# Long convolution with a routed MLP: who applies the filter's decay, products of ones ahead of the first data, and a small first chunk

## The chip, the cores and the metric

One core of one Trainium2 chip runs the program. The metric is the device time of an execution in microseconds (us); less is better. The engines are TensorE (PE in the rows; PEld is its weight load), VectorE (DVE), ScalarE (ACT), GpSimd (POOL) and SyncE (SP), which issues the DMAs.

## What is computed

The reference has two parts. The change lies in the first lines of the first one: the implicit filter.

```python
def _attn_ref(x, v, pos_emb, w1, w2):
    B, S, D = x.shape                                   # 4, 12608, 128
    h_mlp = np.maximum(pos_emb @ w1, 0.0) @ w2          # 64 -> 64 -> 128
    window = np.exp(-0.01 * np.arange(S))[:, None]
    h_filt = h_mlp * window
    u = x * v
    Uf = np.fft.rfft(u, n=2 * S, axis=1)
    Hf = np.fft.rfft(h_filt, n=2 * S, axis=0)
    y = np.fft.irfft(Uf * Hf[None], n=2 * S, axis=1)[:, :S]
    return x * y
```

The second part scores every row of that result with a gate vector, takes the 128 best rows of each batch, sends them through a ReLU MLP (128 to 1024 to 128), scales by the sigmoid of the score and adds them back.

## The kernel before, in words

The positions are laid out on a grid of 111 x 115 (partition, column), so that the transforms become products with small tables of cosines and sines. All products are float32, each of which the trace shows as two MATMUL instructions. The program has four stages: the filter layers (`h_hid`), the filter's spectrum (`h_spec`, 32 groups of four channels, written to a DRAM scratch `hd`), the main loop over 4 x 32 groups with the inverse transform and the row scores, and the routed MLP that runs as background work and at the end.

The order of work is written by hand: each engine runs its instructions in the order in which the code issues them, and the framework adds semaphore waits where two engines touch the same buffer.

`h_hid` is what the change touches. `pos` holds the position embeddings of column j in partitions 0 to 63 and of column j + 58 in partitions 64 to 127, so one product with the block-diagonal table `bw` (L275) makes the hidden layer of both halves. The 58 column pairs are cut into chunks of `PC = 4`: 14 whole chunks and a last one of two. For each chunk:

- L275, PE: first layer, 128 x 444, into one of two PSUM banks (`ps1(k % 2)`, named `a` in the rows).
- L276, ACT: Relu from that bank into `hid`.
- L284, PE: second layer, one product per column and half (64 rows deep, 111 x 128), into a PSUM tile of two banks, `ps2(k % 2)`, named `c`: the first bank for the lower half, the second for the upper.
- L293 and L297, DVE: for the lower half, the product with the decay (plane e = 0 of `hb`) and with the decay and a sign (plane e = 1). `hb` lies in `big` as [111, 2, 128, 115]: column j of a channel is 115 floats from column j of the next.
- L293, DVE, and L295, POOL: for the upper half, DVE makes plane 0, and POOL makes plane 1 from plane 0 with the sign.

The loop issues the first layer and the Relu of chunk k ahead of the second layer and multiplies of chunk k - 1. The DMAs of all chunks are issued at the start on SP's queue (L253), with the tables between them. Ahead of `h_hid`, DVE clears the PSUM banks (L723).

The spectrum begins with `fwd(0)` (`s1`, L228 by way of `mm2`, L221 and L222): 16 products on plane 0 for the lower and upper half, then 16 on plane 1. They need the last chunk's multiplies, on plane 1 those of POOL.

Of the kernel before, what the change touches and what calls it, by code (L numbers as in the profile page):

```python
# [11 lines left out]
AF = mybir.ActivationFunctionType  # L12
ALU = mybir.AluOpType
# [4 lines left out]
B, S, D, FO = 4, 12608, 128, 64  # L18
NQ = 64
N1, N2, N3 = 111, 230, 115  # L20
# [20 lines left out]
PJ = (N3 + 1) // 2  # L41
NC = 2
NS, ND = 64, 4
NWARM = 12
CB = range(2, (NJ + 7) // 8)
PC = 4
# [86 lines left out]
def hyena_moe(ctx, tc, xg, x2, pos, bw, ww, wg, mw1, mw2, c1, gx, cf, ci, wm, tk, out):  # L133
    nc = tc.nc
# [9 lines left out]
    def view(t, off, shape):  # L144
        n = int(np.prod(shape[1:]))
        r = t[:shape[0], off:off + n]
        if len(shape) > 2:
            ax = "abcd"[:len(shape) - 1]
            r = r.rearrange(f"p ({' '.join(ax)}) -> p {' '.join(ax)}", **dict(zip(ax[1:], shape[2:])))
        return r  # L150
# [8 lines left out]
    bank1 = [pp.tile([128, 512], F32, tag=f"a{k}", name=f"a{k}") for k in range(4)]  # L159
    bank2 = [pp.tile([128, 1024], F32, tag=f"c{k}", name=f"c{k}") for k in range(2)]  # L160

    def ps1(k, shape, name):
        return view(bank1[k], 0, shape)

    def ps2(k, shape, name):
        return view(bank2[k], 0, shape)
# [9 lines left out]
    wm_sb = cp.tile([N1, 3, N3], F32, name="wm_sb")  # L176
# [11 lines left out]
    onesb = cp.tile([128, 128], BF16, name="onesb")  # L188
    nc.vector.memset(onesb, 1.0)
    ay = view(big, 0, [128, NG, 2 * NJ, 4])  # L190
    hb = view(big, 0, [N1, 2, D, N3])
# [9 lines left out]
    def load_u(t):  # L201
        b, g = divmod(t, NG)
        if b < B:
            nc.sync.dma_start(buf("u", t, [NP, 2 * XC]), xg[b, :, g])
# [39 lines left out]
    def h_hid():  # L244
        pt, hid = view(arena, POS0, [128, PJ, N1]), view(arena, HID0, [128, PJ, N1])
        wl = view(big, D * 2 * NJ - 256, [128, 2, 128])
        bwt, wwt = wl[:, 0], wl[:, 1]
        nc.sync.dma_start(bwt, bw)
        ch = [(a, min(a + PC, PJ)) for a in range(0, PJ, PC)]

        def load(k):
            a, z = ch[k]
            nc.sync.dma_start(pt[:, a:z], pos[:, a:z])  # L253

        load(0)
        load(1)
        nc.sync.dma_start(wwt, ww)
        nc.sync.dma_start(wm_sb, wm)
        for k in range(2, 5):
            load(k)  # L260
        nc.sync.dma_start(c1_sb, c1)
        nc.sync.dma_start(cf_sb, cf)
        for k in range(5, len(ch)):
            load(k)
        nc.sync.dma_start(ci_sb, ci)
        nc.sync.dma_start(gx_sb, gx)
        nc.sync.dma_start(wgb, wg.partition_broadcast(128))
        nc.sync.dma_start(tk_sb, tk)
        for k in range(NU - 1):
            load_u(k)  # L270
        for k in range(len(ch) + 1):
            if k < len(ch):
                a, z = ch[k]
                hp = ps1(k % 2, [128, PC * N1], f"hid_{k}")[:, :(z - a) * N1]
                nc.tensor.matmul(hp, lhsT=bwt, rhs=pt[:, a:z].rearrange("p j i -> p (j i)"), start=True, stop=True)  # L275
                nc.scalar.activation(out=hid[:, a:z].rearrange("p j i -> p (j i)"), in_=hp, func=AF.Relu)  # L276
            if not k:
                continue
            a, z = ch[k - 1]
            ps = ps2(k % 2, [N1, 2, PC, D], f"hm_{k}")  # L280
            for i in range(z - a):
                for h in range(2):
                    if h * PJ + a + i < N3:
                        nc.tensor.matmul(ps[:, h, i], lhsT=hid[h * FO:(h + 1) * FO, a + i],  # L284
                                         rhs=wwt[h * FO:(h + 1) * FO], start=True, stop=True)
            for h in range(2):
                j0 = h * PJ + a
                j1 = min(h * PJ + z, N3)
                w = j1 - j0
                o = hb[:, :, :, j0:j1]  # L290
                pv = ps[:, h, :w].rearrange("p j d -> p d j")
                wb = wm_sb[:, :, j0:j1].unsqueeze(2).to_broadcast([N1, 3, D, w])
                nc.vector.tensor_tensor(out=o[:, 0], in0=pv, in1=wb[:, 0], op=ALU.mult)  # L293
                if h:
                    nc.gpsimd.tensor_tensor(out=o[:, 1], in0=o[:, 0], in1=wb[:, 1], op=ALU.mult)  # L295
                else:
                    nc.vector.tensor_tensor(out=o[:, 1], in0=pv, in1=wb[:, 2], op=ALU.mult)  # L297

    def h_spec():
        te = {}  # L300
# [363 lines left out]
    def moe(b, ix, ws, mb, ks):  # L664
# [11 lines left out]
        if b + 1 == B:  # L676
            wp = ps1(1, [128, 128], "warm")
            for _ in range(NWARM):
                nc.tensor.matmul(wp, lhsT=ident, rhs=ident, start=True, stop=True)
# [39 lines left out]
        ix = yield from place(b, rk, oh, jio, NJ, 3, ws[:, :128])  # L719
        yield from moe(b, ix, ws, mb, (3, (3, 3, 1, 2)[b]))  # L720

    for t in bank1 + bank2:
        nc.vector.memset(t, 0.0)  # L723
    h_hid()
    o, n, w = OFF["xa"]
    nc.gpsimd.memset(view(arena, o, [128, n * w]), 0.0)
# [7 lines left out]
    for t in range(NT + LAG):  # L734
        g = t % NG
        i = t - LAG
        if 0 <= i:
            f_i(i, sd.pop(i))
        if t < NT:
            p = ps1(2, [128, 512], f"p_{t}")  # L740
# [71 lines left out]
def build(inputs):  # L812
    import concourse.bacc as _bacc
    nc = _bacc.Bacc("TRN2", target_bir_lowering=False, num_devices=1, dynamic_dma_scratch_size=8192)
    arrays, args = {}, []
    for name, a in _layout(inputs):
        arrays[f"in_{name}_dram"] = a
        args.append(nc.dram_tensor(f"in_{name}_dram", a.shape, mybir.dt.from_np(a.dtype), kind="ExternalInput").ap())
    args.append(nc.dram_tensor("out_0_dram", (B, 2 * PR, NJ, D), F32, kind="ExternalOutput").ap())
    with tile.TileContext(nc) as tc:  # L820
        hyena_moe(tc, *args)
    return nc, arrays
# [7 lines left out]
```

## Time and profile before

| | us |
|---|---|
| three runs, median (range) | 1029.34 (1027.65 to 1029.87) |
| the profiled execution | 1029.24 |
| its span, first to last instruction | 1027.3 |
| busy PE / DVE / ACT / POOL | 955.7 / 907.7 / 596.5 / 673.2 |
| mean granted TensorE clock | 0.977 of full |

The profile is of one execution, and the prediction's sums are made against that one. A row of the timeline gives start, duration, engine, line, operation, output and input with shapes, a count when equal instructions that follow each other are merged, and in brackets the idle time before it with what ended it. Starts of instructions on one engine can lie closer than their durations, because the next one begins while the last is still writing. Matmul ends are modelled.

### The profile page before, as it was taken

How to read it: one execution, taken by the hardware profiler on the slowest of the kernel's cores; microseconds unless marked ns; L12 is line 12 of the kernel's file. 1: busy time of each engine (PE TensorE's matmuls, PEld its weight loads, DVE VectorE, ACT ScalarE, POOL GpSimd, SP SyncE). 2: the span in 40 equal slices, each digit the busy share in tenths (PEclk: the TensorE clock that was granted, in tenths of full speed). 3: DMA queues.
4: the chain of work that ended last, by engine and by line, in shares of the span. 5: the costliest groups of instructions: out<-in, count | busy, mean ns of one | idle time of the engine just before them, and what ended most of it. 6: DMA issues, size and time to landing. Idle time of an engine off the chain costs nothing.

```text
span 1027.3 us, 38294 instructions
## 1 busy us (share of the span) xinstructions
PE 955.7 (93%) x15812; PEld 850.5 (83%) x15812; DVE 907.7 (88%) x1559; ACT 596.5 (58%) x1957; POOL 673.2 (66%) x644
## 2 busy tenths in 40 slices
PE   8999989999999999999999999999999999889914
PEld 4788879988888988888889988888899888779903
DVE  7687879999999899999998899999988999996984
ACT  2344435545546887854557878644578876435810
POOL 4800018889887568988975598889845988863500
PEclk9999999999999999999999999999999999999956
DMA  8043366566785866656868765568587655554820
GB/s 234 22 160 152 153 210 199 176 180 196 200 231 180 268 196 179 194 172 184 232 210 270 202 190 172 173 183 243 186 271 220 185 171 178 164 170 127 296 74 5
DMA packets 64785, 190.26 MB, mean 185 GB/s; under 512 B 8693, under 2 KB 15716, under 8 KB 64612
## 3 DMA queue, kind: packets, MB, share of 16 engines
q1 hardware_dynamic: 64356, 187.30, 59.4%
q8 instruction: 124, 2.03, 0.9%
q0 software_dynamic: 256, 0.52, 0.2%
q14 instruction: 49, 0.40, 0.1%
HBM read 146.37 MB, written 41.42 MB: 183 GB/s over the span
## 4 chain that ended last, share of the span: by engine, by line
DVE 47%; PE 39%; issue 6%; DMA 2%; ACT 1%; DVEq 1%; POOLq 0%; SPq 0%; ACTq 0%
PE a L238 10%; PE a L221 9%; DVE arena L348 8%; DVE c L349 8%; PE c L221 7%; DVE c L341 5%; DVE c L340 5%; DVE arena L351 4%; DVE arena L417 4%; PE a L409 4%; DVE arena L350 4%; DVE arena L420 4%; PE a L222 3%; PE c L222 3%; PE c L238 2%
## 5 line engine op out<-in xcount | busy, mean ns | idle before, releaser
L238 PE MATMUL a<-arena,cf_sb 128*64 128x222 f32 x2304 | 260.3, 355 | 15.2 <-DVE c L341 14.3
L357 POOL TENSOR_TENSOR arena<-arena 128x444 f32<-128x444 f32 x127 | 133.7, 1052 | 198.5 <-DVE arena L351 132.4
L230 ACT COPY arena<-a 128x444 f32<-128x444 f32 x288 | 152.2, 530 | 161.5 <-PE a L222 158.5
L221 PE MATMUL c<-ci_sb,arena 128*56 128x116 f32 x2048 | 224.8, 263 | 3.7 <-DVE arena L351 2.5
L222 PE MATMUL c<-ci_sb,arena 128*55 128x116 f32 x2048 | 224.8, 263 | 0.0
L221 PE MATMUL a<-c_sb,arena 111*58 111x111 f32 x2048 | 218.3, 260 | 0.0
L238 PEld LDWEIGHTS a<-arena,cf_sb 128*64 128x64 f32 x2304 | 154.0, 137 | 77.7 <-DVE c L341 46.1
L222 PE MATMUL a<-c_sb,arena 111*57 111x111 f32 x2048 | 218.2, 260 | 0.0
L221 PEld LDWEIGHTS c<-ci_sb,arena 128*56 128x56 f32 x2048 | 207.1, 130 | 4.0 <-issue 2.7
L221 PEld LDWEIGHTS a<-c_sb,arena 111*58 111x58 f32 x2048 | 200.5, 132 | 10.0
L222 PEld LDWEIGHTS c<-ci_sb,arena 128*55 128x55 f32 x2048 | 206.9, 129 | 0.4 <-issue 0.4
L222 PEld LDWEIGHTS a<-c_sb,arena 111*57 111x57 f32 x2048 | 200.4, 131 | 0.2
L409 PE MATMUL a<-big,gx_sb 128*64 128x128 f32 x2880 | 169.8, 273 | 4.5 <-DVE arena L417 3.0
L434 ACT ACTIVATE arena<-arena 128x128 f32<-128x128 f32 x464 | 137.8, 298 | 60.8 <-DVE arena L420 54.7
L409 PEld LDWEIGHTS a<-big,gx_sb 128*64 128x64 f32 x2880 | 159.3, 137 | 8.4 <-DVE arena L417 5.5
L367 ACT COPY big<-c 128x928 f32<-128x928 f32 x128 | 118.3, 924 | 75.1 <-PE c L222 75.1
L210 POOL TENSOR_TENSOR arena<-arena 111x460 f32<-111x460 f32 x128 | 151.4, 1183 | 0.6 <-DMA arena<-in_xg_dram 0.6
L211 POOL TENSOR_TENSOR arena<-arena,wm_sb 111x460 f32<-111x460 f32 x128 | 140.4, 1097 | 10.0
L348 DVE TENSOR_TENSOR arena<-c,arena 128x888 f32<-128x888 f32 x128 | 138.5, 1082 | 7.7 <-DMA arena<-hd 3.4
L349 DVE TENSOR_TENSOR c<-c,arena 128x888 f32<-128x888 f32 x128 | 138.3, 1080 | 0.0
L358 POOL TENSOR_TENSOR arena<-arena 128x444 f32<-128x444 f32 x127 | 135.1, 1064 | 0.0
L393 POOL TENSOR_TENSOR arena<-big 128x256 f32<-128x256 f32 x104 | 90.9, 897 | 65.7 <-PE a L404 64.2
(130 smaller groups left out, 1532.0 us busy)
## 6 DMA issues: line engine op xcount, KB each, us to landing
arena<-hd SPq DMA_DIRECT2D x128, 444.0 KB
arena<-in_xg_dram SPq DMA_DIRECT2D x128, 402.5 KB
arena<-in_x_dram SPq DMA_DIRECT2D x112, 224.0 KB
out_dram<-arena SPq DMA_DIRECT2D x112, 224.0 KB
hd<-arena SPq DMA_DIRECT2D x32, 444.0 KB
arena<-in_moe_w_dram SPq DMA_DIRECT2D x8, 512.0 KB
arena<-in_pos_dram SPq DMA_DIRECT2D x14, 222.0 KB
arena<-in_x_dram SPq DMA_DIRECT2D x8, 112.0 KB
```

What stands on the lines that cost most here:

```text
L210: nc.gpsimd.tensor_tensor(out=u[:, 0], in0=u[:, 0], in1=u[:, 1], op=ALU.mult)
L211: nc.gpsimd.tensor_tensor(out=u[:, 1].rearrange("p (s j) -> p s j", s=4), in0=u[:, 0].rearrange("p (s j) -> p s j", s=4), in1=sg, op=ALU.mult)
L221: nc.tensor.matmul(o[:h], lhsT=lhsT[:, :h], rhs=rhs, **kw)
L222: nc.tensor.matmul(o[NQ:NQ + m - h], lhsT=lhsT[:, h:], rhs=rhs, **kw)
L230: nc.scalar.copy(out=te[:, e], in_=tps[e])
L238: nc.tensor.matmul(pq[w][e * NQ:(e + 1) * NQ, c], lhsT=cf_sb[:, 2 * w + e], rhs=te[:, e, c], start=True, stop=True)
L348: nc.vector.tensor_tensor(out=mt, in0=uv, in1=ht[:, 0].unsqueeze(1).to_broadcast([128, 2, HC]), op=ALU.mult)
L349: nc.vector.tensor_tensor(out=uv, in0=uv, in1=ht[:, 1].unsqueeze(1).to_broadcast([128, 2, HC]), op=ALU.mult)
L357: eng.tensor_tensor(out=nat(sd[:, 0]), in0=nat(yz[:, 0]), in1=rev(yz[:, 1]), op=ALU.add)
L358: eng.tensor_tensor(out=nat(sd[:, 1]), in0=rev(yz[:, 0]), in1=nat(yz[:, 1]), op=ALU.subtract)
L409: nc.tensor.matmul(ps[t * NQ:(t + 1) * NQ, k], lhsT=gx_sb[:, o:o + NQ], rhs=ay[:, :, e * NJ + j], start=e == 0, stop=e == 1)
L434: nc.scalar.activation(out=wx[:, k], in_=wx[:, k], func=AF.Copy, accum_out=self.sc[:, ja + k:ja + k + 1])
```

## The change

The decay of the upper half moves from DVE to ACT. ACT's activation takes one scale per partition, so it handles one column at a time: four instructions per chunk (three in the last). The multiplies of the lower half stay on DVE, POOL still makes plane 1 of the upper half. Ahead of the first chunk PE runs `NWARM0 = 24` products of a bfloat16 tile of ones into bank 3. The chunks are cut so that the first has two columns and the last is whole. For the first chunk the second layer is issued ahead of the next first layer. The clearing of the PSUM banks begins with bank 3.

```diff
+NWARM0 = 24
-        ch = [(a, min(a + PC, PJ)) for a in range(0, PJ, PC)]
+        ch = [(max(a, 0), a + PC) for a in range(PJ % PC - PC, PJ, PC)]
...
-        for k in range(len(ch) + 1):
+        def first(k):
             if k < len(ch):
                 a, z = ch[k]
                 hp = ps1(k % 2, [128, PC * N1], f"hid_{k}")[:, :(z - a) * N1]
                 nc.tensor.matmul(hp, lhsT=bwt, rhs=pt[:, a:z].rearrange("p j i -> p (j i)"), start=True, stop=True)
                 nc.scalar.activation(out=hid[:, a:z].rearrange("p j i -> p (j i)"), in_=hp, func=AF.Relu)
-            if not k:
-                continue
-            a, z = ch[k - 1]
+
+        wp = ps1(3, [128, 128], "warm0")
+        for _ in range(NWARM0):
+            nc.tensor.matmul(wp, lhsT=onesb, rhs=onesb, start=True, stop=True)
+        first(0)
+        for k, (a, z) in enumerate(ch):
+            if k:
+                first(k + 1)
             ps = ps2(k % 2, [N1, 2, PC, D], f"hm_{k}")
...
-            for h in range(2):
-                j0 = h * PJ + a
-                j1 = min(h * PJ + z, N3)
-                w = j1 - j0
-                o = hb[:, :, :, j0:j1]
-                pv = ps[:, h, :w].rearrange("p j d -> p d j")
-                wb = wm_sb[:, :, j0:j1].unsqueeze(2).to_broadcast([N1, 3, D, w])
-                nc.vector.tensor_tensor(out=o[:, 0], in0=pv, in1=wb[:, 0], op=ALU.mult)
-                if h:
-                    nc.gpsimd.tensor_tensor(out=o[:, 1], in0=o[:, 0], in1=wb[:, 1], op=ALU.mult)
-                else:
-                    nc.vector.tensor_tensor(out=o[:, 1], in0=pv, in1=wb[:, 2], op=ALU.mult)
+            if not k:
+                first(1)
+            w = min(PJ + z, N3) - PJ - a
+            o = hb[:, :, :, a:z]
+            pv = ps[:, 0, :z - a].rearrange("p j d -> p d j")
+            wb = wm_sb[:, :, a:z].unsqueeze(2).to_broadcast([N1, 3, D, z - a])
+            for e in range(2):
+                nc.vector.tensor_tensor(out=o[:, e], in0=pv, in1=wb[:, 2 * e], op=ALU.mult)
+            o = hb[:, :, :, PJ + a:PJ + a + w]
+            for i in range(w):
+                nc.scalar.activation(out=o[:, 0, :, i], in_=ps[:, 1, i], func=AF.Copy,
+                                     scale=wm_sb[:, 0, PJ + a + i:PJ + a + i + 1])
+            wb = wm_sb[:, 1, PJ + a:PJ + a + w].unsqueeze(1).to_broadcast([N1, D, w])
+            nc.gpsimd.tensor_tensor(out=o[:, 1], in0=o[:, 0], in1=wb, op=ALU.mult)
...
-    for t in bank1 + bank2:
+    for t in bank1[3:] + bank1[:3] + bank2:
         nc.vector.memset(t, 0.0)
```

In the changed kernel the first layer is L276, the Relu L277, the products of ones L281, the second layer L290, DVE's multiplies L299, ACT's scaling L302 and POOL's product L305.

How the order changes on ACT, from its first Relu on, with the semaphores that each instruction waits for (`PE_49`, `DVE_49`, `Activation_49` are raised by that engine, `DMAHW...` by a DMA; `a0`, `a1` are the banks of the first layer, `c0`, `c1` the tiles of the second). Before:

```order
L187 ACTIVATE gp_90<-one_88 128x1 [waits DVE_49]
L276 ACTIVATE arena_68<-a0_70 128x444 [waits PE_49]
L276 ACTIVATE arena_68<-a1_71 128x444 [waits PE_49]
L276 ACTIVATE arena_68<-a0_70 128x444 [waits PE_49]
L276 ACTIVATE arena_68<-a1_71 128x444 [waits PE_49]
```

And now, in the middle of the filter layers and at their end:

```order
L277 ACTIVATE arena_68<-a1_71 128x444 [waits PE_49]
L302 ACTIVATE big_69<-c0_74,wm_sb_85 111x128 [waits DVE_49,PE_49]
L302 ACTIVATE big_69<-c0_74,wm_sb_85 111x128 x3
L277 ACTIVATE arena_68<-a0_70 128x444 [waits PE_49]
L302 ACTIVATE big_69<-c1_75,wm_sb_85 111x128 [waits DVE_49,PE_49]
L302 ACTIVATE big_69<-c1_75,wm_sb_85 111x128 x3
L302 ACTIVATE big_69<-c0_74,wm_sb_85 111x128 [waits DVE_49,PE_49]
L302 ACTIVATE big_69<-c0_74,wm_sb_85 111x128 x2
```

Between two Relus there are now four scalings, the first of which waits for DVE as well as for PE.

How the order changes on PE, from its first instruction on. Before:

```order
L275 MATMUL a0_70<-arena_68,big_69 128x444 [waits DMAHW1_49,DMAHW0_49,DVE_49]
L275 MATMUL a1_71<-arena_68,big_69 128x444 [waits DMAHW2_49,DVE_49]
L284 MATMUL c1_75<-big_69,arena_68 111x128 [waits DMAHW3_49,DVE_49,Activation_49]
L284 MATMUL c1_75<-big_69,arena_68 111x128 x7
L275 MATMUL a0_70<-arena_68,big_69 128x444 [waits DMAHW5_49]
L284 MATMUL c0_74<-big_69,arena_68 111x128 [waits Activation_49]
```

And now, from the last of the 24 products of ones on:

```order
L281 MATMUL a3_73<-onesb_92 128x128
L276 MATMUL a0_70<-arena_68,big_69 128x222 [waits DMAHW1_49,DMAHW0_49,DVE_49]
L290 MATMUL c0_74<-big_69,arena_68 111x128 [waits DMAHW3_49,DVE_49,Activation_49]
L290 MATMUL c0_74<-big_69,arena_68 111x128 x3
L276 MATMUL a1_71<-arena_68,big_69 128x444 [waits DMAHW2_49]
L276 MATMUL a0_70<-arena_68,big_69 128x444 [waits DMAHW5_49]
L290 MATMUL c1_75<-big_69,arena_68 111x128 [waits DVE_49,Activation_49]
```

The first chunk's second layer now stands ahead of the second chunk's first layer, and two first layers follow each other behind it.

## Rows read from the trace of the kernel before

**Rows 1.** The page, section 1: busy us, share of the span, instructions.
```profile
PE 955.7 (93%) x15812; PEld 850.5 (83%) x15812; DVE 907.7 (88%) x1559; ACT 596.5 (58%) x1957; POOL 673.2 (66%) x644
```

**Rows 2.** Windows: length, busy PE, PEld, DVE, ACT, POOL; PEclk, DMA share, GB/s.
```profile
10.00:15.00 5.00, 5.00 (x53) 3.31 (x50) 4.66 (x9) 1.45 (x3) 2.96 (x3) 1.00 0.98 317
...
50.00:60.00 10.00, 10.00 (x167) 8.98 (x165) 7.50 (x13) 4.83 (x10) 1.09 (x1) 1.00 0.38 150
```

**Rows 3.** Timeline, one steady chunk of the filter layers.
```profile
11.72 1.13 PE L284 MATMUL c<-big,arena 64*111 64x128 f32 x16
11.82 0.54 ACT L276 ACTIVATE arena<-a 128x444 f32<-128x444 f32 x1 [1.46 <-PE a L275]
12.10 1.49 DVE L293 TENSOR_TENSOR big<-c,wm_sb 111x512 f32<-111x512 f32 x2
...
12.78 1.01 PE L275 MATMUL a<-arena,big 128*128 128x444 f32 x2
12.86 1.42 POOL L295 TENSOR_TENSOR big<-big,wm_sb 111x512 f32<-111x512 f32 x1 [0.58 <-DVE big L293]
...
13.50 0.68 DVE L297 TENSOR_TENSOR big<-c,wm_sb 111x512 f32<-111x512 f32 x1
13.72 1.13 PE L284 MATMUL c<-big,arena 64*111 64x128 f32 x16
```

**Rows 4.** Timeline, the start of the program.
```profile
1.15 2.11 DVE L723 MEMSET a<- 128x512 f32 x4
...
4.34 3.30 PE L275 MATMUL a<-arena,big 128*128 128x444 f32 x4 [4.34 <-DMA arena<-in_pos_dram]
...
7.57 1.27 PE L284 MATMUL c<-big,arena 64*111 64x128 f32 x16
...
9.71 1.13 PE L284 MATMUL c<-big,arena 64*111 64x128 f32 x16
```

**Rows 5.** Timeline, the end of the filter layers and the spectrum's first products.
```profile
32.81 0.64 PE L275 MATMUL a<-arena,big 128*128 128x222 f32 x2
...
33.38 1.13 PE L284 MATMUL c<-big,arena 64*111 64x128 f32 x16
33.48 0.36 ACT L276 ACTIVATE arena<-a 128x222 f32<-128x222 f32 x1 [1.09 <-PE a L275]
...
34.96 0.66 PE L284 MATMUL c<-big,arena 64*111 64x128 f32 x6 [0.45 <-DVE big L293]
...
36.68 1.83 POOL L295 TENSOR_TENSOR big<-big,wm_sb 111x512 f32<-111x512 f32 x2 [0.38 <-DVE big L293]
...
37.63 0.30 PE L222 MATMUL a<-c_sb,big 111*57 111x111 f32 x1 [0.23 <-DVE big L293]
...
38.57 0.42 PE L222 MATMUL a<-c_sb,big 111*57 111x111 f32 x1
```

**Rows 6.** Windows, just after the filter layers (columns as in rows 2).
```profile
39.00:41.90 2.90, 2.90 (x34) 2.90 (x33) 0.00 (x0) 0.70 (x2) 2.90 (x1) 0.50 0.00 0
```

**Rows 7.** Timeline, ACT in the main loop, instructions with a per-partition operand.
```profile
366.50 0.39 ACT L570 ACTIVATE ms<-hi,st 128x116 bf16<-128x116 int16 x1
366.80 0.19 ACT L570 ACTIVATION_READ_ACCUMULATOR ms<-hi,st 128x1 bf16 x1
```

**Rows 8.** Groups by line, ACT: busy, mean ns of one, idle before (L585 with, L586 without such operand).
```profile
L585 ACT ACTIVATE st<-st 128x1 f32<-128x1 f32 x6 | 1.8, 295 | 1.8 <-DVE st L576 1.8
L586 ACT ACTIVATE st<-st 128x1 f32<-128x1 f32 x6 | 1.2, 203 | 0.2
```

**Rows 9.** Groups by line, DVE, the same columns.
```profile
L454 DVE TENSOR_TENSOR sc<-sc,tk_sb 128x116 f32<-128x116 f32 x4 | 1.1, 280 | 5.4 <-ACT arena L434 5.4
...
L293 DVE TENSOR_TENSOR big<-c,wm_sb 111x256 f32<-111x256 f32 x1 | 0.4, 429 | 0.0
L293 DVE TENSOR_TENSOR big<-c,wm_sb 111x128 f32<-111x128 f32 x1 | 0.4, 394 | 0.0
```

**Rows 10.** Timeline, PE's weight loads of 24 float32 products near the program's end.
```profile
1013.35 5.08 PEld L679 LDWEIGHTS a<-ident 128*128 128x128 f32 x24 [0.30 <-issue]
```

## The prediction

> **What bounds the kernel now.** I read the page's busy shares first: TensorE (PE) is busy 93% of the span, VectorE (DVE) 88%, ScalarE (ACT) 58% [rows 1]. That average says little about a change that touches only the filter layers, so next come the stages. From 10 to 15 us, in the filter layers, PE is busy 5.00 of 5.00 us and ACT 1.45; right after the filter, from 50 us, PE is again busy 10.00 of 10.00 [rows 2]. So a microsecond won or lost before the filter spectrum begins moves everything behind it.
>
> The timeline of one steady chunk [rows 3] shows what paces the filter layers. The second-layer products (L284) start at 11.72 and at 13.72: 2.00 us per chunk. Of that, 1.06 us are the sixteen second-layer matmuls (11.72 to 12.78) and 0.94 us the two first-layer ones (12.78 to 13.72). PE never pauses; DVE, with three multiplies of 0.69, 0.68 and 0.69 us at a pitch of about 0.60, fits beside it; ACT does one 0.54 us Relu. **PE is the bound, DVE just under it.** A chunk is ready for DVE 1.18 us after its L284 starts (11.72 to 12.90, where the second multiply of the pair that begins at 12.10 starts: 12.10 + 1.49 - 0.69). I call that moment "ready". POOL starts 0.07 us after the upper-half multiply ends (12.10 + 0.69 to 12.86), my price for a hop between engines.
>
> At the front [rows 4] the first product waits until 4.34 for its data. The four first-layer matmuls then take 3.30 us, 0.82 each, where a later pair takes 0.94 with the change to the next kind of product: half the pace, so 1.2 GHz, although this stretch is recorded as full. L284 of the first two chunks starts at 7.57 and 9.71.
>
> At the end [rows 5] the last whole chunk's L284 starts at 33.38 (ready 34.56). The spectrum's first products with an upper half start at 37.63, after DVE's last multiply, and those that need POOL's part at 38.57, after POOL ends at 38.51 (36.68 + 1.83). PE had been nearly idle from 35.6 (34.96 + 0.66) to 37.6; from 38.5 to 41.9 the granted clock is 0.50, that is 1.2 GHz [rows 6], which costs half of 3.4, 1.7 us.
>
> **The change part by part.**
>
> *DVE's third multiply* (0.69 us, 15 of them) goes. PE, the bound, does the same 58 first-layer columns and 230 second-layer matmuls as before, so by itself this frees nothing: the pace cannot fall under 2.00.
>
> *ACT's position-by-position scaling.* Four instructions of 128 elements per chunk. Price from both sides: a contiguous instruction of 116 elements with a per-partition operand lets the next start after 0.30 us (366.50 to 366.80) [rows 7], and such an operand costs 0.09 (295 against 203 ns for one element) [rows 8]. These write side by side; the scaling writes one float per 460 bytes. The only row with that write pattern is DVE's last multiply, 111x128 into one column: 394 ns, where DVE takes 280 for 116 contiguous elements, some 290 for 128 [rows 9]. So a column write costs 0 to 0.10 us more. I take 0.10, since that row is the same tile at the same stride: pitch p = 0.40, duration 0.48. Lower end p = 0.30, duration 0.38; still lower, p = 0.20, if the operand were free.
> On this the Trainium skill, "SBUF — State Buffer", section "Door 1", says that accesses which cross to a new 16-byte line each time pay a penalty and that two hits on a line are needed for full rate; it names no price for ACT. By it every scaling would pay; without it the lower end holds. DVE's rows agree: two floats per line, 429 ns for 256 elements, lie on the line of the contiguous ones, one float per line does not.
>
> *The wait the change adds.* This is the term that decides. In the built program the first scaling of a chunk waits for the DVE count that only the second lower-half multiply of the same chunk raises (both engines read one PSUM tile); the order of ACT shows the wait. Behind that scaling, in ACT's queue, stands the Relu of the chunk after next, and PE's L290 of that chunk waits for this Relu. So there is a loop over two chunks: ready(k), two multiplies 0.60 + 0.68 = 1.28, hop 0.07, four scalings 4p, Relu 0.54, hop 0.07, L290 1.18, ready(k+2): 3.14 + 4p. PE needs 4.00 for two chunks. With p = 0.40 the loop takes **4.74 us for two chunks, 2.37 each**; with 0.30, 4.34; only under p = 0.215 does PE stay the bound.
>
> *Front.* The first chunk is half as wide (two positions) and its data should land some 0.4 us earlier (111 KB less at 250 to 300 GB/s), but the 24 products of ones stand before it on PE. They start near 1.7 (first memset, 1.15 + 0.49). The nearest row, 24 float32 products of the same size at the low level, takes 5.08 us, 0.21 each [rows 10]; bfloat16 should need one pass for two, so I take half, 2.5 us, and 5.1 as upper bound. They end at 4.2; the first product starts at 4.3, as before, but at 2.4 GHz. Then: Relu starts 0.67 later and takes 0.36 (33.48 after 32.81) [rows 5], hop, L290 at 5.40; eight matmuls 0.64; both next first-layer products 0.74 + 0.94; L290 of chunk 1 at 7.72, ready(1) = 8.90. Before, the chunk of that number was ready at 9.71 + 1.18 = 10.89: **2.0 us won** (it lay two positions further on, which the tail counts). The data of chunk 2 is needed at 6.8 instead of 8.77, which looks just in time.
>
> *Loop.* ready(13) = 8.90 + 6 x 4.74 = 37.34, against 34.56: the gain is spent and 2.8 us more.
>
> *Tail.* The last chunk is now whole (four lower, three upper positions) and comes through the same loop. ready(12) = 8.90 + 5 x 4.74 + 2.00 = 34.60; its scalings let the last Relu start at 37.55; L290 at 38.16, ready 39.2, multiplies to 40.5, three scalings to 41.8, POOL 1.06 us (three quarters of 1.41) to 43.0. Against 38.57: **+4.4 us**. PE idles from 39.1 to 41.8, so I expect a half-speed stretch as before; as part of it may fall into PE's own waiting, up to 0.9 us of it may cost nothing. Sum +3.5 to +4.4, taken as +4.0.
>
> *At no cost:* the new memset order (the bank PE needs first comes first; DVE then idles until 6), GpSimd's new broadcast (same elements, 1.41 us per chunk under 2.37).
>
> The sum is against the profiled execution, 1029.24 us (span 1027.3 and 1.9 around it), 0.1 under the median of 1029.34. Forecast 1029.2 + 4.0 = **1033.2 us**. A measurement here can tell about 0.2%, 2.1 us, from no change.
>
> **The rivals.**
> A is the forecast: loop with column writes dear.
> B, not slower: the same loop, but ACT writes columns as fast as contiguous data (p = 0.30). ready(13) = 8.90 + 6 x 4.34 = 34.94, the same tail ends at 40.3: +1.75, less up to 0.9 of hidden half speed: 1030.5. For it: ACT's own rows show no dear access; against it, DVE's column. It decides by p: under about 0.32 the front's gain pays for the loop to within 0.2%.
> C, faster: the loop does not bind (p under 0.215, or the scaling rarely waits). PE keeps 2.00: ready(13) = 32.9, the spectrum's second products start between 36.7 and 38.0 instead of 38.57, and if PE's shorter idle keeps 2.4 GHz, 1.7 us more is saved: 1025.7 to 1028.7, say 1027.2. Against it: the wait stands in the program, and the row with an operand and one element lasts 0.295.
> D, worse: the products of ones last 5.1 us. The first data waits until 6.8 and A's end moves by up to 2.5: 1035.7. For it only the float32 row.
> That the change does not do what it says is excluded by the order: 15 DVE rows fewer, 57 ACT rows more.
>
> **How the numbers follow.** A 0.56, B 0.31, C 0.07, D 0.06. A comes before B because the row with the same write pattern pays. Range 1029.5 to 1035.6: below lie C and the low edge of B (with its hidden half speed), above lies D. A alone: 1031.5 to 1034.5. Slower by over 0.2%: A but for its low edge, D, and a tenth of B, 0.61; within 0.2%: most of B, 0.33; faster: most of C, 0.06.
>
> **What would show it.** L290 starts 2.37 apart on average, alternating about 2.0 and 2.7; ACT's scaling starts right after DVE's second multiply and PE waits for L277; scalings near 0.48 us at pitch 0.40; the spectrum's products near 41.8 and 43.0; first L276 near 4.3, L290 of chunk 1 near 7.7. Scalings of 0.38 us make it B; L290 every 2.00 us makes it C, and the forecast wrong.

## The result, and the profile after

The changed kernel takes **1035.6 us** (median of 6 runs, 1033.72 to 1038.28) beside 1029.24 (6 runs, 1027.65 to 1032.2): ratio **1.0061 [1.0041, 1.008]**, slower by 6.4 us. The forecast was 1033.2 us, slower, range 1029.5 to 1035.6: the sign is right, the time lies exactly on the upper end of the range, and some of the terms are wrong in ways that partly cancel. The profiled execution took 1034.75 us, span 1032.8, so profile against profile there are 5.5 us to account for.

First the page's busy shares of the changed kernel, which answer to [rows 1]. DVE gave up 10.2 us, ACT took 15.7:

```profile
PE 961.8 (93%) x15836; PEld 854.4 (83%) x15836; DVE 897.5 (87%) x1544; ACT 612.2 (59%) x2014; POOL 673.1 (65%) x644
```

Then the windows, to be read beside [rows 2] and [rows 6] (columns as there). In the filter layers PE is no longer full, 4.82 of 5.00 us, and the stretch at the half level (granted clock 0.50, that is 1.2 GHz) is longer: 41 to 47 us, where before it was 39.0 to 41.9.

```profile
25.00:30.00 5.00, 4.82 (x50) 3.18 (x52) 2.96 (x5) 3.56 (x11) 3.70 (x3) 1.00 0.01 2
...
40.00:41.00 1.00, 0.11 (x2) 0.00 (x0) 0.26 (x1) 0.65 (x3) 1.00 (x1) 0.85 0.00 0
41.00:42.00 1.00, 0.57 (x6) 0.57 (x8) 0.00 (x0) 0.38 (x2) 0.67 (x2) 0.50 0.00 0
42.00:47.00 5.00, 5.00 (x58) 5.00 (x56) 0.00 (x0) 1.06 (x2) 5.00 (x3) 0.50 0.01 3
47.00:48.00 1.00, 1.00 (x13) 0.89 (x11) 0.00 (x0) 0.36 (x1) 0.92 (x2) 0.73 0.00 0
```

The timeline of two chunks, to be read beside [rows 3]:

```profile
24.93 1.13 PE L290 MATMUL c<-big,arena 64*111 64x128 f32 x16
25.48 1.28 ACT L302 ACTIVATE big<-c,wm_sb 111x128 f32<-111x128 f32 x4 [0.60 <-DVE big L299]
25.99 1.01 PE L276 MATMUL a<-arena,big 128*128 128x444 f32 x2
26.11 1.29 DVE L299 TENSOR_TENSOR big<-c,wm_sb 111x512 f32<-111x512 f32 x2 [0.72 <-PE c L290]
26.52 0.61 ACT L277 ACTIVATE arena<-a 128x444 f32<-128x444 f32 x1
...
27.18 1.13 PE L290 MATMUL c<-big,arena 64*111 64x128 f32 x16 [0.18 <-ACT arena L277]
27.49 1.29 ACT L302 ACTIVATE big<-c,wm_sb 111x128 f32<-111x128 f32 x4 [0.36 <-DVE big L299]
...
29.20 0.47 PE L290 MATMUL c<-big,arena 64*111 64x128 f32 x3
```

L290 starts at 24.93, 27.18 and 29.20: gaps of 2.25 and 2.02, alternating, **4.27 us for two chunks** instead of 4.00. The loop stands in the rows: DVE's two multiplies end at 27.40 (26.11 + 1.29), ACT's scalings start at 27.49, released by DVE; the next Relu follows 1.04 us after such a start (25.48 to 26.52), so four scalings take **0.26 each**; the Relu takes 0.61; and PE resumes at 27.18, released by that Relu. The groups by line and the waits of the first 46 us give the sums:

```profile
L302 ACT ACTIVATE big<-c,wm_sb 111x128 f32<-111x128 f32 x57 | 18.5, 496 | 8.4 <-DVE big L299 8.4
L277 ACT ACTIVATE arena<-a 128x444 f32<-128x444 f32 x14 | 8.4, 600 | 3.4 <-DVE big L299 3.1 <-PE a L276 0.3
```
```profile
DVE big L299 <- PE c L290: 13.5, 14, 2.6
...
PEld c L290 <- ACT arena L277: 10.8, 13, 1.1
...
ACT big L302 <- DVE big L299: 8.4, 14, 1.9
```

A scaling lasts 496 ns, but the next one starts after 260: duration and pitch differ by almost two. DVE now idles 13.5 us waiting for products, and ACT 8.4 us for DVE: both have time, and each waits.

The start, beside [rows 4]:

```profile
1.69 2.72 PE L281 MATMUL a<-onesb 128*128 128x128 bf16 x24 [1.69 <-DVE a L731]
...
4.20 1.06 PE L276 MATMUL a<-arena,big 128*128 128x222 f32 x2
...
5.70 1.20 PE L290 MATMUL c<-big,arena 64*111 64x128 f32 x8 [0.44 <-ACT arena L277]
...
7.93 0.78 DVE L299 TENSOR_TENSOR big<-c,wm_sb 111x256 f32<-111x256 f32 x2 [2.53 <-DMA wm_sb<-in_wm_dram]
8.40 0.50 PEld L276 LDWEIGHTS a<-arena,big 128*128 128x128 f32 x2 [1.08 <-DMA arena<-in_pos_dram]
...
10.11 1.13 PE L290 MATMUL c<-big,arena 64*111 64x128 f32 x16
```

The products of ones last 2.72 us, near the 2.5 assumed, and the first layer starts at 4.20. But it takes 1.06 for 222 columns, where [rows 5] show 0.64, and eight L290 take 1.20, where experiment 5 below shows 0.69. By this pace PE is still at 1.2 GHz, although the windows record a granted clock of 1.00 from 0 to 10 us; what is said below of the level at the start is read from the pace in the same way. The data of chunk 2 come at 8.40, and L290 of chunk 1 starts at 10.11.

The end, beside [rows 5]:

```profile
35.73 1.13 PE L290 MATMUL c<-big,arena 64*111 64x128 f32 x16 [0.19 <-ACT arena L277]
...
37.73 1.12 PE L290 MATMUL c<-big,arena 64*111 64x128 f32 x14 [0.88 <-ACT arena L277]
...
38.97 1.29 DVE L299 TENSOR_TENSOR big<-c,wm_sb 111x512 f32<-111x512 f32 x2 [0.77 <-PE c L290]
...
40.35 1.03 ACT L302 ACTIVATE big<-c,wm_sb 111x128 f32<-111x128 f32 x3 [0.78 <-DVE big L299]
41.43 0.44 PE L223 MATMUL a<-c_sb,big 111*57 111x111 f32 x1 [1.32 <-ACT big L302]
...
41.46 1.24 POOL L305 TENSOR_TENSOR big<-big,wm_sb 111x384 f32<-111x384 f32 x1 [0.34 <-ACT big L302]
...
42.95 0.39 PE L223 MATMUL a<-c_sb,big 111*57 111x111 f32 x1
```

PE's last L290 ends at 38.85; then DVE, ACT and POOL follow one another, 38.97 to 42.70, while PE stands nearly idle. The products on plane 1 start at 42.95 (the ninth L223; POOL ended at 42.70), where before it was 38.57.

The spectrum's second group (output `c`), by source line, first of the kernel before and then of the changed one (count, durations, first and last start):

```profile
L238 PE MATMUL c<-arena,cf_sb x256: 348/350/402, 45.4 to 136.7; 128*64 128x222 f32 x128
```
```profile
L239 PE MATMUL c<-arena,cf_sb x256: 347/350/402, 50.3 to 141.6; 128*64 128x222 f32 x128
```

**The account**, from landmark to landmark: front, second chunk's L290 at 10.11 against 9.71, +0.40; twelve more chunks, 25.62 against 23.67 us, +1.95, of which 1.6 is the loop (0.135 per chunk) and the rest the new cut, since before the last of these steps had only half a first layer in it (1.63 us, from 31.75 to 33.38); from there to plane 1's products, 7.22 against 5.19, +2.03; to the second group, 7.35 against 6.83, +0.5, with some 4.6 us of it at the half level against 3.3; together 4.9. The other 0.6 comes behind the main loop, where nothing was changed: from the second group to the main loop's last L238 or L239 (916.1 and 920.8) the two take 870.7 and 870.5 us, from there to the end 111.2 and 112.0. Both stretches vary by more than that over the profiles of this study, 869 to 872 and 110.7 to 114.1 us.

### The profile page after: what moved, and what is told of

Read it like the earlier page. It is cut to its first block, busy times and chain, and to the rows that moved or that the text cites. A ratio compares the mean times of both kernels' runs of the same rounds, so it can differ in the third digit from the quotient of the medians.

```text
span 1032.8 us, 38405 instructions
## 1 busy us (share of the span) xinstructions
PE 961.8 (93%) x15836; PEld 854.4 (83%) x15836; DVE 897.5 (87%) x1544; ACT 612.2 (59%) x2014; POOL 673.1 (65%) x644
## 3 DMA queue, kind: packets, MB, share of 16 engines
q8 instruction: 125, 2.05, 0.9%
## 4 chain that ended last, share of the span: by engine, by line
PE 52%; DVE 32%; issue 5%; DMA 5%; ACT 1%; SPq 1%; POOL 0%; DVEq 0%; POOLq 0%; ACTq 0%
PE a L239 14%; PE a L222 12%; PE c L222 11%; DVE arena L356 5%; DVE c L357 5%; PE a L417 4%; DVE arena L425 3%; PE a L223 3%; DVE c L349 3%; DVE c L348 3%; PE c L223 3%; DVE arena L359 3%; DMA arena<-in_x_dram 3%; DVE arena L428 3%; PE c L239 2%
## 5 line engine op out<-in xcount | busy, mean ns | idle before, releaser
L239 PE MATMUL a<-arena,cf_sb 128*64 128x222 f32 x2304 | 261.8, 356 | 14.7 <-DVE c L349 13.7
L223 PE MATMUL c<-ci_sb,arena 128*55 128x116 f32 x2048 | 226.1, 264 | 0.9 <-issue 0.9
L239 PEld LDWEIGHTS a<-arena,cf_sb 128*64 128x64 f32 x2304 | 154.0, 137 | 78.8 <-DVE c L349 48.0
L223 PE MATMUL a<-c_sb,arena 111*57 111x111 f32 x2048 | 216.9, 259 | 0.0
L223 PEld LDWEIGHTS c<-ci_sb,arena 128*55 128x55 f32 x2048 | 208.0, 130 | 0.0
L223 PEld LDWEIGHTS a<-c_sb,arena 111*57 111x57 f32 x2048 | 199.2, 131 | 0.1
## 6 DMA issues: line engine op xcount, KB each, us to landing
arena<-in_x_dram SPq DMA_DIRECT2D x8, 112.0 KB
```

The lines of the kernel that those rows point to most:

```text
L223: nc.tensor.matmul(o[NQ:NQ + m - h], lhsT=lhsT[:, h:], rhs=rhs, **kw)
L239: nc.tensor.matmul(pq[w][e * NQ:(e + 1) * NQ, c], lhsT=cf_sb[:, 2 * w + e], rhs=te[:, e, c], start=True, stop=True)
```

## The experiments

Each was timed beside the kernel before on the same chip. Several chips took part, so runs of different groups are compared by their ratios. All keep the changed kernel's other parts unless the text says otherwise.

**1. A PSUM tile of its own for the upper half**, so that ACT and DVE no longer read one tile.

```diff
-ps = ps2(k % 2, [N1, 2, PC, D], f"hm_{k}")
+ps = (ps2(k % 2, [N1, PC, D], f"hm_{k}"), ps1(2 + k % 2, [N1, PC, D], f"hu_{k}"))
...
-                nc.scalar.activation(out=o[:, 0, :, i], in_=ps[:, 1, i], func=AF.Copy,
+                nc.scalar.activation(out=o[:, 0, :, i], in_=ps[1][:, i], func=AF.Copy,
```

> The change with one edit: the upper half's second-layer products go to a PSUM tile of their own, so that ACT's scaling no longer waits for DVE's second multiply. Theory (the wait and the Relu queued behind the scaling set the pace): from the second chunk on L290 starts every 2.00 us instead of 4.27 for two, so L290 of the last whole chunk comes 6 x 0.27 = 1.6 us earlier counted from chunk 1; the spectrum's first full products come some 3 us earlier after that, and the whole ends 3 to 5 us under the change, 1030 to 1032.5. Rival (ACT's column writes or its load set the pace, whatever it waits for): L290 keeps about 2.13 per chunk and the whole stays within 1.5 us of the change.

Measured: 1029.49 us (10 runs), ratio 1.0001 [0.9991, 1.0012]. ACT's timeline in this run:

```profile
27.07 1.29 ACT L302 ACTIVATE big<-a,wm_sb 111x128 f32<-111x128 f32 x4 [0.34 <-PE a L290]
28.11 0.61 ACT L277 ACTIVATE arena<-a 128x444 f32<-128x444 f32 x1
29.07 1.29 ACT L302 ACTIVATE big<-a,wm_sb 111x128 f32<-111x128 f32 x4 [0.35 <-PE a L290]
```

The scalings start every 2.00 us, released by PE, at the same pitch of 0.26 (1.04 to the Relu). With the scalings and their column writes still there the loss is gone, to within the interval: **the loss hangs on the wait for DVE**. At the end of the filter layers seven scalings run without a wait for DVE, and plane 1's products start at 39.17:

```profile
35.08 2.06 ACT L302 ACTIVATE big<-a,wm_sb 111x128 f32<-111x128 f32 x7 [0.34 <-PE a L290]
...
L239 PE MATMUL c<-arena,cf_sb x256: 348/350/402, 44.3 to 135.6; 128*64 128x222 f32 x128
```

In this profile the granted clock stays at 1.00 from 36 to 48 us, so the half-level stretch is gone as well, and the second group starts at 44.3, 6.0 us earlier than in the changed kernel. How much of that each execution would show is open; the time of ten runs is what carries the result.

**2. The upper half's decay as one DVE multiply**, in the new cut and with the products of ones: the change without its ACT part.

```diff
-            for i in range(w):
-                nc.scalar.activation(out=o[:, 0, :, i], in_=ps[:, 1, i], func=AF.Copy,
...
+            nc.vector.tensor_tensor(out=o[:, 0], in0=ps[:, 1, :w].rearrange("p j d -> p d j"), in1=wd, op=ALU.mult)
```

> The change with the upper half's decay back on DVE as one multiply per chunk; products of ones, small first chunk and the new order stay. Theory: no scaling stands ahead of the Relu, L290 starts every 2.00 us; but the last chunk is whole and DVE has three multiplies for it and three for the one before, so the spectrum's second products start some 5 us after the last whole chunk's L290 of 34.1, about 40; total 1030 to 1032. Rival (front and tail cost most of the loss, not the scaling): within 1.5 us of the change, 1034 to 1037.

Measured: 1031.73 us (10 runs), ratio 1.0022 [1.0008, 1.0036]. L290 every 2.00 us, and still slower than before: front and cut by themselves gain nothing, they cost about 0.2%. In its profile PE ran at half pace until 13 us in spite of the products of ones (L290 of the second chunk, at 11.01, took 2.05 us); the upper half's first product started at 40.80, since DVE's three multiplies of the whole last chunk ended at 40.75.

**3. ACT's scaling alone**: old cut, old order, no products of ones, one tile.

```diff
-                nc.vector.tensor_tensor(out=o[:, 0], in0=pv, in1=wb[:, 0], op=ALU.mult)
...
+            for i in range(w):
+                nc.scalar.activation(out=o[:, 0, :, i], in_=ps[:, 1, i], func=AF.Copy,
+                                     scale=wm_sb[:, 0, PJ + a + i:PJ + a + i + 1])
```

> The kernel before with ACT's scaling alone; old chunks, no products of ones, old order and clearing. Theory: the loop of 4.27 us for two chunks stands here too, and costs 0.135 x 12 = 1.6 us up to the last whole chunk; the last chunk of two positions keeps the tail short (about +0.5). Total 1030.5 to 1032.5, 1.5 to 3 us over before. Rival (the scaling costs nothing, the loss is front and tail of the new cut): within 1 us of before.

Measured: 1033.22 us (5 runs), ratio 1.0037 [1.0023, 1.0052], a little above the range expected. Its timeline has the same loop, 4.27 us from 25.48 to 29.75:

```profile
25.48 1.13 PE L284 MATMUL c<-big,arena 64*111 64x128 f32 x16 [0.19 <-ACT arena L276]
25.78 1.28 ACT L294 ACTIVATE big<-c,wm_sb 111x128 f32<-111x128 f32 x4 [0.35 <-DVE big L291]
...
27.49 1.13 PE L284 MATMUL c<-big,arena 64*111 64x128 f32 x16
...
29.75 1.13 PE L284 MATMUL c<-big,arena 64*111 64x128 f32 x16 [0.19 <-ACT arena L276]
```

**4. The change without its products of ones.**

```diff
-NWARM0 = 24
+NWARM0 = 0
```

> The change without the products of ones. Theory: in the change's profile they did not raise the clock before 10 us, so without them the first product starts when its data lands, some 0.2 us earlier, and the rest is as in the change: total within 1 us of it, L290 of chunk 1 at 9.5 to 10.3. Rival (they bring 2.4 GHz earlier in most executions): 1 to 2 us slower than the change, L290 of chunk 1 later than 10.5.

Measured: 1034.94 us (5 runs), ratio 1.0045 [1.0028, 1.0061], which overlaps the changed kernel's 1.0061 [1.0041, 1.008]. A gain from the products does not show, nor a loss. In its profile PE ran at half pace until about 13 us, and L290 of chunk 1 started at 11.35 instead of the 9.5 to 10.3 expected; with the products it came between 9.84 (experiment 1) and 11.01 (experiment 2), so one execution does not tell.

**5. The scalings of chunk k issued behind the next Relu**: the tile and the wait for DVE stay, only ACT's queue changes.

```diff
         for k, (a, z) in enumerate(ch):
             if k:
                 first(k + 1)
+                scale(k - 1, ps)
...
+        scale(len(ch) - 1, ps)
```

> The changed kernel with the multiplies and scalings of chunk k written behind the first layer of chunk k+2, so that on ScalarE the next Relu goes ahead of the scalings; the PSUM tile of two banks and the wait of the scalings for VectorE stay. Theory (what paces the loop is the Relu queued behind the waiting scalings): the L290 starts go from 4.27 us per two chunks to 4.00, as with a tile of its own; 14 chunks give 14 x 0.13 = 1.9 us; the tail keeps its wait (last lower multiplies 1.28, then scalings 1.04, then POOL 1.24), so the time lies near 1033.6 us (1032.6 to 1034.6). Rival (the banks are given back too late: multiplies 1.28 + scalings 1.04 behind the products leave no room, whatever the queue order): the pace stays above 4.15 us per two chunks and the time at 1034.8 us or more.

Measured: 1032.87 us (6 runs), ratio 1.004 [1.0025, 1.0055], 0.2% under the changed kernel, though the intervals overlap, so the time alone does not tell; the profile does for the pace: L307 (its second layer) starts every 2.00 us.

```profile
27.54 1.13 PE L307 MATMUL c<-big,arena 64*111 64x128 f32 x16
27.64 0.54 ACT L277 ACTIVATE arena<-a 128x444 f32<-128x444 f32 x1 [0.28 <-PE a L276]
28.08 1.28 ACT L294 ACTIVATE big<-c,wm_sb 111x128 f32<-111x128 f32 x4
...
29.54 1.13 PE L307 MATMUL c<-big,arena 64*111 64x128 f32 x16
```

The pace is repaired by queue order alone, so what made the loop was **the Relu standing behind waiting scalings**. Two thirds of the loss stay: 1.004 here against 1.0001 with a tile of its own. The end shows where: the same wait, where no later chunk hides it. In experiment 1 the last scalings do not wait for DVE; here the last three start 1.38 us after the start of DVE's last multiplies (36.65), and PE resumes only behind them, at 39.11 instead of 37.19 in experiment 1. After that the granted clock is 0.50 until about 45.5 us, where in experiment 1 it stayed at 1.00.

```profile
38.03 1.03 ACT L294 ACTIVATE big<-c,wm_sb 111x128 f32<-111x128 f32 x3 [0.64 <-DVE big L291]
```
```profile
39.11 0.43 PE L223 MATMUL a<-c_sb,big 111*57 111x111 f32 x1 [1.32 <-ACT big L294]
```

**6. Experiment 3 with tiles of their own**: the kernel before with ACT's scaling and these tiles, nothing else.

```diff
-            ps = ps2(k % 2, [N1, 2, PC, D], f"hm_{k}")
+            ps = (ps2(k % 2, [N1, PC, D], f"hm_{k}"), ps1(2 + k % 2, [N1, PC, D], f"hu_{k}"))
```

> The kernel before with ScalarE's scaling alone, the upper half in PSUM tiles of its own; old chunks (short one last), no products of ones. Theory: L284 starts every 2.00 us as before, since TensorE paces; at the end VectorE has two multiplies per chunk instead of three, so L284 of the last chunk no longer waits 0.45 for VectorE, and the first spectrum product with the upper half starts at 36.5 instead of 37.63, the one that needs POOL at 37.8 instead of 38.57: 0.8 to 1.1 us less than before, 1028.3 us (1027.8 to 1029.2). Rival (scalings, Relus and POOL are late by as much as VectorE was; or the clock falls in the tail as it did before): 1029.4 us, no difference from before; if old chunks are worse than the short first chunk, slower than the run with tiles of its own and the changed kernel's chunks, 1029.5 us.

Measured: 1028.07 us (12 runs), ratio 0.999 [0.998, 1.0]: not slower than before, at most 0.2% faster. The upper half's first product starts at 36.23 instead of 37.63. Experiments 3 and 6 differ in the tile alone: 0.5%.

**7. The products of ones alone**, in the kernel before; eight more behind each of the first two first-layer products, and the banks cleared in the changed kernel's order.

```diff
+        ones(24)
         for k in range(len(ch) + 1):
...
+            if k < 2:
+                ones(8)
```

> The kernel before with products of ones alone: 24 ahead of the first layer as in the change, and 8 more behind each of the first two first-layer products, so that TensorE idles less until about 8.8 us. Old order, VectorE multiplies. Theory (in the changed kernel the products did not bring the granted clock to 2.4 GHz before 10 us because TensorE idled again behind them; and much of the front waits for data): if with the gaps filled the full level comes by about 6 us, L284 of the second chunk starts at 8.7 to 9.2 instead of 9.71 and the time is 0.5 to 1.0 us less, 1028.6 us. Rival (the products, filled or not, do not move when the level rises, or the start waits for data anyway): L284 of the second chunk at 9.7 or later, the products behind the first layer cost up to 0.9 us each on TensorE's queue; 1029.4 to 1030.5 us.

Measured: 1030.23 us (12 runs), ratio 1.0008 [0.9995, 1.0022]. PE's rows:

```profile
4.21 1.04 PE L282 MATMUL a<-arena,big 128*128 128x444 f32 x2
...
6.88 1.13 PE L293 MATMUL c<-big,arena 64*111 64x128 f32 x16
9.41 1.01 PE L282 MATMUL a<-arena,big 128*128 128x444 f32 x2 [1.41 <-DMA arena<-in_pos_dram]
10.36 1.13 PE L293 MATMUL c<-big,arena 64*111 64x128 f32 x16
```

Here the products did what the forecast took for granted: the first layer runs at 2.4 GHz from 4.21 (1.04 for 444 columns). And it gains nothing, because PE then stands for 1.41 us at the third chunk's data, with the second chunk's second layer behind it in its queue: that starts at 10.36, where 8.7 to 9.2 was expected.

**8. As 7, with the loads of `ww` and `wm` issued from ACT's queue**, so that SP reaches the third chunk earlier.

```diff
-        nc.sync.dma_start(wwt, ww)
-        nc.sync.dma_start(wm_sb, wm)
+        nc.scalar.dma_start(wwt, ww)
+        nc.scalar.dma_start(wm_sb, wm)
```

> The run of products of ones alone, with the two loads of the second layer's weights and of the mask table issued from ScalarE's queue instead of SP's, so that SP issues the third chunk's data at about 2.1 us instead of 3.0. Theory (with the ones the granted clock is up by about 5 us, and what then holds the start is the third chunk's data: L282 of it waited 1.41 us for its load and started at 9.41): L282 of the third chunk starts at 8.4 to 8.9, L293 of the second chunk at 9.4 to 9.8 instead of 10.36, the time 0.5 to 1.0 us under the run of ones alone: 1029.2 to 1029.7 us. Rival (the loads are held by what the memory delivers, 250 to 313 GB/s between 5 and 8 us, not by SP's issues): the third chunk's data still come at 9.2 or later and the time stays at 1030.2 us.

Measured: 1030.7 us (12 runs), ratio 1.0004 [0.999, 1.0018]. The theory fell: the third chunk no longer waits, but the first two do, and the first layers start at 4.74 and 7.70, where experiment 7 had 4.21 and 5.53. In the first 5 us and the next 5 much the same is moved in both profiles (133 and 259 GB/s in experiment 7, 143 and 241 here): this fits loads that share what is delivered, where the order of issue only decides which one is late. The Trainium skill, "Trainium Kernel Development and Optimization", "Key Constraints", says that DMAs of several queues run on the same 16 DMA engines, so that more queues save only the time of issuing; this run agrees, as no more was moved.

```profile
4.74 1.82 PE L282 MATMUL a<-arena,big 128*128 128x444 f32 x2 [0.34 <-DMA arena<-in_pos_dram]
...
7.70 0.98 PE L282 MATMUL a<-arena,big 128*128 128x444 f32 x2 [0.28 <-DMA arena<-in_pos_dram]
```

**9 to 11. Combinations on top of experiment 6**: with 7 and 8; with 12 products of ones in the idle time after the last second layer; with all of it.

```diff
+        for _ in range(12):
+            nc.tensor.matmul(wt, lhsT=onesb, rhs=onesb, start=True, stop=True)
     def h_spec():
```

> ScalarE's scaling with PSUM tiles of its own in the old chunks (1028.07 us), with the products of ones (24, and 8 behind each of the first two first-layer products) and the two loads on ScalarE's queue. Theory (front held by the third chunk's data, which come earlier): L284 of the second chunk at 9.2 to 9.6 instead of 9.71 and 0.1 to 0.5 us less, 1027.6 to 1028.0 us. Rival (ones behind the first-layer products put work on TensorE's queue and the data still come late): 1028.1 to 1029.0 us.

> ScalarE's scaling with PSUM tiles of its own in the old chunks (1028.07 us), with 12 products of ones behind the last second-layer product, where TensorE otherwise idles for 1.0 us before the spectrum starts. Theory (the half-level stretch of 38.6 to 41.7 us in that run follows from the idle time before it, and costs about 1.6 us): with the idle time filled the granted clock stays at 1.00 from 36 to 46 us and the time is 1.0 to 1.6 us less, 1026.5 to 1027.1 us. Rival (the fall comes all the same, from the wait for POOL or from what went before): a stretch at 0.50 remains, 1028.0 to 1028.5 us.

> The two runs before together: tiles of its own, old chunks, products of ones at the start and at the end, two loads on ScalarE's queue. Theory: the gains of both add, 1026.0 to 1027.1 us, under the kernel before by 2 to 3 us. Rival (one or both of them gain nothing): 1027.6 to 1028.6 us.

Measured, 12 runs each: 1028.67 us, ratio 0.9986 [0.9972, 1.0001]; 1027.62, 0.9979 [0.9965, 0.9993]; 1027.17, 0.9974 [0.996, 0.9988]. The first lies in the range of its rival, the other two between theory and rival. The second profile kept the level at 1.00 from 34 to 48 us. So did the first, though without products at the end, so that these products hold the level is not shown; the intervals overlap.

**12. Everything but the moved loads, and the second chunk's second layer ahead of the third chunk's first.**

```diff
+        for k in range(2):
+            first(k)
+        for k in range(2):
+            second(k)
+        first(2)
+        for k in range(2, len(ch)):
+            first(k + 1)
+            second(k)
```

> Tiles of its own, old chunks, products of ones at the start and at the end as in the run of all together (1027.17 us), with the loads back on SP's queue, and with the second-layer products of the second chunk written ahead of the first layer of the third, whose data come at 8.4 to 9.4 us. Theory (what keeps the front from using the higher clock is TensorE standing at the late data with work behind it that is ready): the second layer of the second chunk starts at 7.8 to 8.4 us instead of 9.5 to 10.4, the idle time of TensorE between 7 and 10 us falls under 0.5 us, and the time is 0.7 to 1.2 us less, 1026.0 to 1026.5 us. Rival (the time lost at the data is only moved: the first layers of the third and fourth chunk then stand in a row with their Relus, or the data set the pace of all early chunks): 1027.0 us or more.

Measured: **1025.52 us** (6 runs, 1023.01 to 1026.62), ratio **0.9952 [0.9933, 0.9971]**: 0.5% under the kernel before and 1.1% under the changed one. PE's timeline:

```profile
5.96 0.96 PE L283 MATMUL a<-arena,big 128*128 128x444 f32 x2
...
9.57 1.76 PE L283 MATMUL a<-arena,big 128*128 128x444 f32 x4 [0.26 <-DMA arena<-in_pos_dram]
11.87 0.36 PE L294 MATMUL c<-big,arena 64*111 64x128 f32 x1 [0.54 <-ACT arena L284]
```

The wait at the data shrinks from 1.41 us to 0.26, as expected. But part of the time is only moved, as the rival had it, and by the mechanism of this case: ACT's scalings of the first two chunks wait for `wm` until 9.12, the next two Relus (L284) stand behind them, and PE waits 0.54 us for the first of these. ACT's timeline:

```profile
9.12 2.32 ACT L304 ACTIVATE big<-a,wm_sb 111x128 f32<-111x128 f32 x8 [1.62 <-DMA wm_sb<-in_wm_dram]
11.18 1.06 ACT L284 ACTIVATE arena<-a 128x444 f32<-128x444 f32 x2
```

The third chunk's second layer starts at 11.87: half a microsecond ahead of experiment 7 (12.36), but not ahead of the kernel before (11.72 [rows 3]), and 0.1 us ahead of experiment 10 (11.99), which has no edit at the front. So the profile shows no gain from the front. The spectrum's second group starts at 43.2 (experiment 10: 43.3, the kernel before: 45.4); that lead is made at the end of the filter layers, where the tiles of their own shorten the chain and the granted clock stayed at 1.00 to 48 us. What this profile has over that of experiment 10 behind this point, 1024.7 us of span against 1029.4, lies in the main loop (869.3 against 872.0) and after it (112.2 against 114.1), where nothing was changed. The intervals of the two ratios overlap, so that the new order pays is not shown, and 2 to 3 us of the measured 0.5% have no cause in the rows.

## Why the forecast was right, and where it was wrong

**The added wait and its loop: right.** DVE's multiplies, ACT's scalings, the Relu behind them and PE's L290 close a loop longer than PE's 4.00 us, as the forecast said; experiments 1, 5 and 6 undo it in two ways, and the pace goes back to 2.00 each time. That this wait "is the term that decides" holds for the end of the filter layers too.

**The price of a scaling: wrong.** The step was "a column write costs 0 to 0.10 us more. I take 0.10 ...: pitch p = 0.40, duration 0.48". The duration was right, 0.496; the pitch was not, 0.26, under the chosen value and under the lower end from the contiguous row, though above the 0.20 that the prediction gave for a free operand. In a queue of independent instructions it is the pitch that counts, and DVE's row gave a duration. With 0.26, and 0.61 for a Relu behind a scaling, the forecast's own sum is 3.14 + 1.04 + 0.07 = 4.25; measured 4.27. Over six pairs this made the loop 2.8 us too long. On the Trainium skill's "SBUF — State Buffer", "Door 1": the runs show the column-writing scalings 0.1 us longer than the contiguous instruction of [rows 7] (0.50 against 0.39) and no slower in succession (0.26 against 0.30); they agree with a penalty at most in the duration. The two instructions differ in size, type and source as well, and no run wrote the scalings side by side, so that the column writes make the difference is not shown.

**The front's 2.0 us: wrong.** That the first product starts "at 4.3, as before, but at 2.4 GHz" and that the data of chunk 2 "looks just in time" at 6.8 both failed: the pace was the lower one, and the data came at 8.40. L290 of chunk 1 started at 10.11 instead of 7.72. Experiment 7 tells the two apart: even where the level is up at 4.2, the late data take the gain; in experiment 5, level up as well (L276 of half a chunk in 0.75), L276 of chunk 2 waits 1.54 us and starts at 8.57. The forecast timed the landing of the first load and assumed that of the third.

**The tail: right by cancellation.** 41.8 and 43.0 were forecast for the spectrum's products, 41.43 and 42.95 came: 2.8 us too much in the loop against 2.4 too little in the front, and a tail 0.4 longer than summed (POOL took 1.24 us for 384 elements, not 1.06, and the products on plane 0, at the half level, ran 0.25 us past its end). Its mechanism, the last chunk whole and passed from DVE to ACT to POOL, was the forecast's.

**The half level: wrong in sign.** Up to 0.9 us was to cost nothing. Instead the stretch lasted until about 47.5, and +0.5 us came with it. That and 0.6 us further on, which no run attributes, carry the profile past the 4.0 us of the sum to 5.5, and the medians lie 6.4 apart.

**The rivals.** B's price (0.30) was the nearer one, yet its time was not reached, since it shared the front's error. C, a loop that doesn't bind, is what the change becomes with tiles of their own: 1029.49, above C's 1025.7 to 1028.7, as L290 of chunk 1 comes late there too (9.84 against 7.72); with the old cut as well (experiment 6) it is 1028.07. D is excluded by the row of 2.72 us.

## What to carry to other kernels

Before moving work to an idle engine, ask what it will wait for there and what stands behind it in that queue: two engines reading one PSUM tile were ordered one after the other, and a Relu behind the waiting scalings cost the pace of the whole stage. A buffer of its own per reader, or writing the wait behind the urgent instruction, returns the pace; only the former also shortens the end of the stage. Warming or speeding the front can pay only as far as the data have landed; here no run shows that it paid. Putting ready work ahead of the instruction that waits for data took that wait from 1.41 us to 0.26, and the same queue, scalings ahead of a Relu, took part of it back.

## What was not expected of the hardware

- The scalings with one-column writes: 496 ns each, one every 260 ns.
- When the level rises at the start, read from PE's pace, varies between executions of like instruction streams. With 24 products of ones ahead, the first layers ran at full pace from 4.2 us in experiments 5 and 7, from about 10 in the changed kernel and from 13 in experiment 2; without any, from about 7.8 in the kernel before and from about 13 in experiment 4. The windows record 1.00 for all these stretches. One profile cannot tell what the products do to it.
- POOL's product of 512 elements takes 1.48 us in the new cut (1478 ns on average) and 1.41 in the old one [rows 3], with ACT or DVE ahead of it alike; the cut changes only the column at which a chunk begins.
